# Reordering the start, the late modulation and the last attention heads of a fused adaLN attention and SwiGLU kernel

## Chip, cores and metric

The kernel runs on one core of one Trainium2 chip. The metric is device time in microseconds (us): the median of several executions. The profile of one execution gives the span, which is 1.8 us shorter than the timed value, and the start and duration of every instruction. It also records which share of its clock TensorE was granted; in these traces that is 1.0 or 0.5. TensorE is called PE, its weight loads PEld, VectorE DVE, ScalarE ACT, GpSimd POOL, and the queue that issues the transfers SP. An eviction is the copy of a finished result out of PSUM, where matmuls leave it; a load has landed when its data is there.

## The reference, cut to what matters

```python
mod = (silu(c) @ w_mod).reshape(1, 6, 1, -1)          # w_mod: 1024 x 6144
sa, ca, ga, sb, cb, gb = [mod[:, i] for i in range(6)]
h = layernorm(x) * (1 + ca) + sa                      # x: 2048 x 1024
q = h @ wq                                            # 32 heads of 128
#   softmax(q k^T / sqrt(128)) v over the last 512 cache rows, 4 kv heads
x = x + ga * (attention @ wo)
h = layernorm(x) * (1 + cb) + sb
x = x + gb * ((silu(h @ w_gate) * (h @ w_up)) @ w_down)   # 3584 wide
```

Here `s` stands for shift, `c` for scale and `g` for gate. Only `sa` and `ca` (16 columns of 128) are needed before the first query matmul. The other four (32 columns, "late modulation") are needed later: `ga` when the first chunk's attention is projected back, the rest only in the FFN.

## The kernel before

Rows are handled in four chunks of 512. Attention is one loop over 4 x 32 heads. In iteration i, PE projects the query of head i (`qproj`), computes the scores of head i-1, and multiplies the probabilities of head i-2 with V (`pv`); ACT does the exponentials between. After the last head of a chunk, `oproj` multiplies with `wo`. Every instruction goes through a helper that sets its semaphore waits in program order, and all transfers are issued by SP, one after the other.

The start: the modulation weights of `sa` and `ca` arrive as eight row blocks; row blocks of x are normalised and transposed between them; then the modulation is applied, and only head 0 is projected before the loop starts.

```python
for t in range(TPC):
    stats(t, t, 0); stats(t, t, 1); aggr(t)
    if t > 0:
        norm(t - 1, t - 1, t - 1)
        x_first(t - 1)
        mod_mm(wme[:, t - 1, :], B_wme[t - 1], t - 1, NE, XB)
# ... remaining blocks, mod_read, mod_gain, warm(4), modulate ...
qproj(0)
```

The late modulation: `ga` is done in chunk one with its own buffer. The rest goes through one single buffer in chunk two (heads 34 to 57), a load every third head, used two heads later.

```python
wml = h2s0[:, :, :].rearrange("p a b -> p (a b)")[:, 0:NL * P]      # the one buffer
def load_wml(k):
    T.op(Q_wml, lambda: SP.dma_start(wml, w_mod[k * P:(k + 1) * P, (NE + DT) * P:]), writes=[B_wml])
# ... in the loop over heads, at the head of iteration i ...
kk, odd = divmod(i - Hq - 2, 3)
if odd == 0 and 0 <= kk < DT:
    load_wml(kk)
if odd == 2 and 0 <= kk < DT:
    mod_mm(wml, B_wml, kk, NL, XB)          # 24 matmuls of one column
    # ... after the last: read, gain, row of gb ...
# ... if i > 0: qproj(i);  scores(i - 1);  pv(i - 2);  run_bg(1) ...
```

`run_bg` advances a background task, the layer norm of the next chunk. That task too issues transfers on SP: a DMA transpose of each normalised row block (L396), which waits for DVE. So does `pv`: it ends with a DMA transpose of the head's output (L567), which waits for its eviction by DVE.

The softmax here doesn't subtract the row's maximum and nothing guards it: scores larger than these inputs give would overflow.

Of the kernel before, what the change touches and what calls it, by code (L numbers as in the profile page):

```python
# [130 lines left out]
def bass_adaLN_cond__sliding_block_cached__swiglu_ffn__prompt_kernel(  # L131
# [49 lines left out]
    ident = S_("ident", [P, P], BF16)  # L181
    ones_bf = S_("ones_bf", [P, P], BF16)
# [7 lines left out]
    zwarm = S_("zwarm", [P, 512], BF16)  # L190
    rowb = [S_("rowb%d" % i, [P, D], BF16) for i in range(2)]
    diag = [S_("diag%d" % i, [P, P], BF16) for i in range(4)]
# [6 lines left out]
    h2s0 = S_("h2s0", [P, DT, CH], BF16)  # L199

    KB = 1024
    A_BYTES = 152 * KB
# [5 lines left out]
    ps_t = ps.tensor  # L208

# [14 lines left out]
    B_ident = _Buf("ident"); B_ones = _Buf("ones"); B_mh = _Buf("mhalf")  # L224
    B_cT = _Buf("cT"); B_sc = _Buf("sc"); B_modbf = _Buf("modbf"); B_c6 = _Buf("c6")
    B_mode = _Buf("mode"); B_modga = _Buf("modga"); B_gf = _Buf("gf"); B_zw = _Buf("zw")
    B_g = [_Buf("g%d" % i) for i in range(2)]
    B_row = [_Buf("row%d" % i) for i in range(2)]
    B_diag = [_Buf("diag%d" % i) for i in range(4)]
# [19 lines left out]
    with nc.Block() as block:  # L249

        @block.gpsimd
        def _(g):
# [9 lines left out]
            def transpose(out_ap, in_ap, reads, bank_buf):  # L262
                T.op(PE, lambda: TE.transpose(out_ap, in_ap, ident[:, :]),  # L263
                     reads=reads + [B_ident], writes=[bank_buf])
# [16 lines left out]
            T.op(POOL, lambda: g.memset(ident[:, :], 0.0), writes=[B_ident])  # L281
            T.op(POOL, lambda: g.affine_select(out=ident[:, :], in_=ident[:, :], compare_op=ALU.not_equal,
                                               fill=1.0, base=0, pattern=[[-1, P]], channel_multiplier=1),
                 reads=[B_ident], writes=[B_ident])
            T.op(POOL, lambda: g.memset(ones_bf[:, :], 1.0), writes=[B_ones])
            T.op(POOL, lambda: g.memset(mhalf[:, :], -0.5), writes=[B_mh])
            T.op(POOL, lambda: g.memset(zwarm[:, :], 0.0), writes=[B_zw])
# [25 lines left out]
            OFF_OS = 148 * KB  # L313
            OFF_KN = OFF_EX

            NE = 2 * DT
            B_wme = [_Buf("wme%d" % k) for k in range(DT)]
            wme = arena.at(OFF_OT, [DT, NE * P], BF16, [])
            arena.regs.append((OFF_OT, OFF_OT + 32 * KB, B_wme))
            Q_wm = [dq("q_wm%d" % k) for k in range(DT)]  # L320
            for k in range(DT):
                T.op(Q_wm[k], lambda: SP.dma_start(wme[:, k, :], w_mod[k * P:(k + 1) * P, 0:NE * P]), writes=[B_wme[k]])  # L322

            NWQ = 2
            B_wq = [_Buf("wq%d" % i) for i in range(NWQ)]
            wq_s = [arena.at(OFF_WQ + i * 8 * KB, [DT, 512], BF16, [B_wq[i]]) for i in range(NWQ)]
# [3 lines left out]
            def load_wq(gidx):  # L330
                if gidx >= NCH * HG:
                    return
                sl = gidx % NWQ
                hg = gidx % HG
                T.op(Q_wq[sl], lambda: SP.dma_start(  # L335
                    wq_s[sl], A_wq[:, hg * 512:(hg + 1) * 512].rearrange("(k p) n -> p k n", p=P)), writes=[B_wq[sl]])

            load_wq(0)
            B_kn = [_Buf("kn%d" % i) for i in range(Hkv)]
            B_kT = _Buf("kT"); B_va = _Buf("va")  # L340
            k_nat = arena.at(OFF_KN, [GK, P], BF16, B_kn)
            kT_sb = arena.at(OFF_KT, [GK, P], BF16, [B_kT])
# [5 lines left out]
            for gk in range(Hkv):  # L348
                T.op(Q_k[gk], lambda: SP.dma_start(k_nat[:, gk * KT:(gk + 1) * KT, :],
                                                   A_k_cache[0, gk, Sk - W:Sk, :].rearrange("(p k) d -> p k d", p=P)),  # L350
                     writes=[B_kn[gk]])
            for gk in range(Hkv):
# [4 lines left out]
            load_wq(1)  # L357
# [23 lines left out]
            def modulate(dst, bufs, dt, gi, ccol, cbuf):  # L381
                T.op(DVE, lambda: V.tensor_scalar(dst[:, dt, :], dst[:, dt, :], gain[gi][:, dt:dt + 1],  # L382
                                                  mod_bf[:, ccol + dt:ccol + dt + 1], op0=ALU.mult, op1=ALU.add),
                     reads=[B_g[gi], cbuf, bufs[dt]], writes=[bufs[dt]])
# [27 lines left out]
            def mod_mm(w_ap, wbuf, k, n, b):  # L412
                for j in range(n):
                    mm(bank(b, 1, 2 * j), w_ap[:, j * P:(j + 1) * P], sc_bf[:, k:k + 1],
                       k == 0 and j == 0, k == DT - 1, [wbuf, B_sc], PB[b], skip=True)

            def mod_read(b, jt0, n, cbuf):
                T.op(DVE, lambda: V.tensor_copy(mod_bf[:, jt0:jt0 + n], psap(b * 512, [[2, n]])),
                     writes=[PB[b], cbuf])

            def mod_gain(gi, jt, cbuf):
                T.op(DVE, lambda: V.tensor_scalar(gain[gi][:, :], mod_bf[:, jt:jt + DT], 1.0, None, op0=ALU.add),
                     reads=[cbuf], writes=[B_g[gi]])

            def warm(n):
                for _ in range(n):
                    mm(bank(QB), zwarm[:, 0:P], zwarm[:, :], True, True, [B_zw], PB[QB])


            def x_first(t):  # L430
                for dt in range(DT):
                    transpose(bank_bf(t)[:, dt * P:(dt + 1) * P], nsc4[t][:, dt * P:(dt + 1) * P], [B_ns4[t]], PB[t])
                T.op(ACT, lambda: A.activation(hT[0][:, :, t * P:(t + 1) * P],
                                               bank_bf(t).rearrange("p (a b) -> p a b", a=DT), AF.Copy),
                     writes=[PB[t]] + B_hT[0])

            for t in range(TPC):
                stats(t, t, 0)
                stats(t, t, 1)
                aggr(t)  # L440
                if t > 0:
                    norm(t - 1, t - 1, t - 1)
                    x_first(t - 1)
                    mod_mm(wme[:, t - 1, :], B_wme[t - 1], t - 1, NE, XB)
            norm(TPC - 1, TPC - 1, TPC - 1)
            x_first(TPC - 1)
            for k in range(TPC - 1, DT):
                mod_mm(wme[:, k, :], B_wme[k], k, NE, XB)
            mod_read(XB, 0, NE, B_mode)
            mod_gain(0, DT, B_mode)  # L450
            modulate(hT[0], B_hT[0], 0, 0, 0, B_mode)
            T.op(DVE, lambda: V.tensor_copy(gain_f[:, :], gain[0][:, :]), reads=[B_g[0]], writes=[B_gf])
            warm(4)
            for dt in range(1, 5):
                modulate(hT[0], B_hT[0], dt, 0, 0, B_mode)
            for dt in range(5, DT):
                T.op(ACT, lambda: A.activation(hT[0][:, dt, :], hT[0][:, dt, :], AF.Identity,
                                               bias=mod_bf[:, dt:dt + 1], scale=gain_f[:, dt:dt + 1]),
                     reads=[B_gf, B_mode, B_hT[0][dt]], writes=[B_hT[0][dt]])


            B_wga = [_Buf("wga%d" % k) for k in range(DT)]
            wga = arena.at(OFF_WO + 48 * KB, [DT, D], BF16, B_wga)
            Q_wga = [dq("q_wga%d" % i) for i in range(2)]

            def load_wga(i):
                hk = DT // 2
                T.op(Q_wga[i], lambda: SP.dma_start(
                    wga[:, i * hk:(i + 1) * hk, :],
                    w_mod[i * hk * P:(i + 1) * hk * P, NE * P:NE * P + D].rearrange("(k p) n -> p k n", p=P)),  # L470
                     writes=B_wga[i * hk:(i + 1) * hk])


            NL = NJ - NE - DT
            B_wml = _Buf("wml")
            Q_wml = dq("q_wml")
            for b_ in B_h2[0]:
                b_.absorb(B_wml)
            wml = h2s0[:, :, :].rearrange("p a b -> p (a b)")[:, 0:NL * P]

            def load_wml(k):
                T.op(Q_wml, lambda: SP.dma_start(wml, w_mod[k * P:(k + 1) * P, (NE + DT) * P:]), writes=[B_wml])


            def row_task(ri, jt, cbuf):
                T.op(POOL, lambda: g.tensor_copy(c6[:, jt:jt + DT], mod_bf[:, jt:jt + DT]), reads=[cbuf], writes=[B_c6])

                def diags(n):
                    for q in range(4):
                        col = jt + 4 * n + q  # L490
                        T.op(POOL, lambda: g.tensor_scalar(diag[q][:, :], ident[:, :], c6[:, col:col + 1], None, op0=ALU.mult),  # L491
# [4 lines left out]
                for n in range(2):  # L496
                    for q in range(4):
                        mm(bank(XB, P, q * P), ones_bf[:, :], diag[q][:, :], q == 0, q == 3, [B_ones, B_diag[q]], PB[XB], skip=True)
# [7 lines left out]
            NQT = 3; NEX = 2; NOS = 4  # L506
# [6 lines left out]
            def qproj(i):  # L513
# [4 lines left out]
                for kc in range(DT):  # L518
                    mm(bank(QB), wq_s[sl][:, kc, hh * P:(hh + 1) * P], hT[ch % 2][:, kc, :], kc == 0, kc == DT - 1,
                       [B_wq[sl], B_hT[ch % 2][kc]], PB[QB])  # L520
# [3 lines left out]
            qproj(0)  # L524
            for idx in range(GK):
                b = PVB + idx // 8
                transpose(bank_bf(b)[:, (idx % 8) * P:(idx % 8 + 1) * P], k_nat[:, idx, :], [B_kn[idx // KT]], PB[b])
            for bi in range(2):
                T.op(DVE, lambda: V.tensor_copy(kT_sb[:, bi * 8:bi * 8 + 8, :],
                                                bank_bf(PVB + bi).rearrange("p (a b) -> p a b", a=8)),  # L530
                     writes=[PB[PVB + bi], B_kT])
# [6 lines left out]
            def scores(i):  # L538
# [4 lines left out]
                for kt in range(KT):  # L543
                    mm(bank(SCB + kt), kT_sb[:, gk * KT + kt, :], qT_s[qs], True, True, [B_kT, B_qT[qs]], PB[SCB + kt])
# [43 lines left out]
            def oproj(ch):  # L588
                for k in range(2 * TPC):
                    j, hf = divmod(k, 2)  # L590
                    t = ch * TPC + j
                    b = [QB, XB][k % 2]
                    for h in range(Hq):
                        mm(bank(b), oT_all[:, h, j * P:(j + 1) * P], wo_s[h // 4][:, h % 4, hf * 512:(hf + 1) * 512],
                           h == 0, h == Hq - 1, [B_wo[h // 4], B_oT[h]], PB[b])
# [201 lines left out]
```

## Time and profile before

| | before |
|---|---|
| median of 4 runs | 1315.57 us (1314.04 to 1316.74) |
| span of the profiled run | 1314.7 us |
| PE busy | 97% |
| one 128x512 matmul to the next at full clock | 0.2157 us |
| the same with the clock not granted | 0.427 us |
| one 129-column matmul to the next | 0.0586 us |

PE is almost always busy, so the busy share says little. These are lines of the page of the kernel before: the span, busy times (share, instructions), and the granted clock of PE in 40 slices (9 is 90% or more).

```profile
span 1314.7 us, 18053 instructions
PE 1280.9 (97%) x7776; PEld 653.6 (50%) x7776; DVE 451.0 (34%) x827; ACT 339.0 (26%) x379; POOL 37.2 (3%) x92
PEclk9999999999999999999999999999999999999999
...
PE 94%; DMA 5%; SPq 1%; issue 0%; DVE 0%; ACT 0%; DVEq 0%
```

The last line is the chain of work that ended last, by engine. The 5% of DMA in it are the clue: something on PE waits for loads. The list of waits of PE in the kernel before shows which (total us, times, longest):

```profile
PE ps L259 <- DMA h2s<-in_w_mod_dram: 16.3, 7, 4.4
PE ps L263 <- DVE nsc L377: 8.0, 1, 8.0
PE ps L259 <- DMA arena<-in_w_mod_dram: 3.6, 4, 1.6
PE ps L259 <- DVE arena L564: 1.1, 1, 1.1
PE ps L259 <- DMA arena<-in_A_wq_dram: 0.7, 1, 0.7
PE ps L259 <- ACT arena L546: 0.4, 1, 0.4
```

The first line is the late modulation in its single buffer (`h2s`), the second the wait for the first normalised block at the start. The same by stretches of time, kernel before; columns are the stretch, its length, busy us (instructions) of PE, PEld, DVE, ACT and POOL, granted clock, DMA share and GB/s:

```profile
0.00:40.00 40.00, 27.21 (x270) 16.90 (x271) 16.70 (x35) 15.55 (x17) 5.10 (x18) 1.00 0.99 318
40.00:205.00 165.00, 165.00 (x1191) 91.66 (x1190) 70.13 (x136) 63.11 (x62) 8.29 (x17) 1.00 0.60 145
205.00:312.00 107.00, 90.66 (x815) 53.24 (x814) 45.18 (x94) 45.02 (x44) 4.68 (x12) 0.94 0.64 147
...
```

After the start, the stretch 205 to 312 is the only long one with an idle PE, and the only one with a clock below 1 (312 to 630, left out, is 318.00 busy of 318.00 at 1.00). The clock record of this trace begins with the first grant, at 27.43 us, so the 1.00 of the first row does not show the slow matmuls before it. A busy sum does not show the slow matmuls, so I used a finer account: every matmul is charged its interval at full clock (0.2157 us for 512 columns, 0.0586 for 129, 0.057 for a 128-column transpose, 0.025 for one column), and what lies between two starts beyond that is "lost". In stretches without stalls this account loses almost nothing: 0.01 us in the 165 us from 40 to 205 us. For the kernel before it gives 1266 us of pure matmul work and 48 us lost.

These are lines of SP and PE of the kernel before (start, us, what, wait before it and its cause):

```profile
220.87 0.75 PE L259 MATMUL ps<-sc_bf,h2s 128*128 128x1 bf16 x24 [2.10 <-DMA h2s<-in_w_mod_dram]
...
229.11 1.26 SPq L396 DMA_TRANSPOSE arena<-nsc  x1
230.46 0.53 SPq L335 DMA_DIRECT2D arena<-in_A_wq_dram  x1
231.04 0.63 SPq L482 DMA_DIRECT2D h2s<-in_w_mod_dram  x1
...
238.33 0.75 PE L259 MATMUL ps<-sc_bf,h2s 128*128 128x1 bf16 x24 [4.43 <-DMA h2s<-in_w_mod_dram]
```

The buffer is free at 221.6 us, but the next load is issued at 231.0 us. Before it in the queue stand the transpose of a head's output (L567, issued at 227.82 us after its wait for DVE), the transpose of the layer norm (L396) and a 1 MB load of `wq` (L335). It lands at 238.28 us, 7.2 us after its issue and 4.4 us after PE wanted it.

This is the start of the kernel before on PE (start, us, what, wait before it and its cause):

```profile
8.03 1.03 PE L263 MATMUL ps<-ident,nsc 128*128 128x128 bf16 x8 [8.03 <-DVE nsc L377]
...
20.01 1.87 PE L259 MATMUL ps<-zwarm 128*128 128x512 bf16 x4
22.62 3.59 PE L259 MATMUL ps<-arena 128*128 128x512 bf16 x8 [0.74 <-DMA arena<-in_A_wq_dram]
...
27.58 6.59 PE L259 MATMUL ps<-arena 128*128 128x512 bf16 x41
```

The eight query matmuls of head 0 take 3.59 us, 0.43 us each: the clock is not granted yet.

### The profile page before, as it was taken

The page shows a single profiled execution, that of the slowest core. Times are in us where ns is not written, and L with a number is a line of the kernel's source. Part 1 is how long each engine was busy: PE and PEld are TensorE (multiplying, and loading weights), DVE is VectorE, ACT ScalarE, POOL GpSimd, SP SyncE. Part 2 cuts the span into 40 slices and gives each one's busy share as a digit, 9 for nine tenths or more (in the row PEclk, how much of TensorE's full clock was granted, in tenths as well). Part 3 has the DMA queues.
Part 4 walks back from the last instruction along what each step waited for, and adds up shares of the span by engine and source line. Part 5 has one row for each costly group of instructions (what it writes and reads, how often), then busy time and mean ns, then how long its engine had stood idle before and what let it go on. Part 6 is the DMA issues. An engine that isn't in the chain of part 4 may idle for free.

```text
span 1314.7 us, 18053 instructions
## 1 busy us (share of the span) xinstructions
PE 1280.9 (97%) x7776; PEld 653.6 (50%) x7776; DVE 451.0 (34%) x827; ACT 339.0 (26%) x379; POOL 37.2 (3%) x92
## 2 busy tenths in 40 slices
PE   6999999879999999999999999999999999999999
PEld 3666545445545665455654444444444444444444
DVE  4555224444225543155431332223212332222112
ACT  3555204444204553045530111001110111001100
POOL 1010000001000000000000000000000000000000
PEclk9999999999999999999999999999999999999999
DMA  9998403775204643036460496025620574035400
GB/s 312 219 246 227 111 0 89 161 168 117 53 1 105 124 101 88 1 73 151 102 141 17 145 302 194 11 86 154 199 65 24 152 209 128 16 111 162 129 9 24
DMA packets 210560, 155.33 MB, mean 118 GB/s; under 512 B 104752, under 2 KB 195760, under 8 KB 210480
## 3 DMA queue, kind: packets, MB, share of 16 engines
q1 hardware_dynamic: 210480, 154.17, 44.2%
q8 instruction: 61, 1.00, 0.3%
q14 instruction: 19, 0.16, 0.0%
HBM read 125.83 MB, written 4.19 MB: 99 GB/s over the span
## 4 chain that ended last, share of the span: by engine, by line
PE 94%; DMA 5%; SPq 1%; issue 0%; DVE 0%; ACT 0%; DVEq 0%
PE ps L259 93%; DMA h2s<-in_w_mod_dram 3%; DMA arena<-in_A_wq_dram 1%; DMA arena<-in_B_w_up_dram 1%; SPq L322 0%; SPq L396 0%; PE ps L263 0%; SPq L302 0%; SPq L335 0%; ACT arena L546 0%; DVE arena L564 0%; DVE nsc L377 0%; SPq L683 0%; DVE tmp L583 0%; DVE arena L585 0%
## 5 line engine op out<-in xcount | busy, mean ns | idle before, releaser
L259 PE MATMUL ps<-arena 128*128 128x512 bf16 (+1 forms) x6428 | 1071.0, 329 | 2.3 <-DVE arena L564 1.1
L259 PEld LDWEIGHTS ps<-arena 128*128 128x128 bf16 x6428 | 549.7, 98 | 520.0 <-issue 9.2
L546 ACT ACTIVATE arena<-ps 128x1024 bf16<-128x1024 f32 x256 | 261.8, 1023 | 386.9 <-PE ps L259 375.2
L727 ACT ACTIVATE arena<-ps 128x512 bf16<-128x512 f32 x112 | 66.9, 597 | 520.2 <-PE ps L259 520.2
L259 PE MATMUL ps<-h2s,arena 128*128 128x512 bf16 x896 | 194.1, 379 | 0.3 <-DMA arena<-in_B_w_up_dram 0.3
L728 DVE TENSOR_TENSOR arena<-ps,arena 128x512 bf16<-128x512 f32 x112 | 77.5, 692 | 276.9 <-PE ps L259 276.9
L583 DVE TENSOR_TENSOR tmp<-ps,rowb 128x512 f32<-128x512 f32 (+1 forms) x65 | 44.4, 683 | 327.5 <-PE ps L259 327.5
L259 PEld LDWEIGHTS ps<-h2s,arena 128*128 128x128 bf16 x896 | 87.5, 98 | 106.5 <-DMA arena<-in_B_w_up_dram 1.3
L522 DVE CAST arena<-ps 128x512 bf16<-128x512 f32 x128 | 88.5, 692 | 92.8 <-PE ps L259 92.8
L564 DVE TENSOR_TENSOR arena<-ps,rl 128x512 bf16<-128x512 f32 x128 | 88.5, 691 | 4.6 <-DVE rl L561 0.2
L561 DVE RECIPROCAL rl<-ps 128x4 f32<-128x4 f32 x128 | 23.4, 183 | 143.6 <-PE ps L259 143.6
L366 DVE BATCH_NORM_STATS2 st<-x_res 128x6 f32<-128x512 bf16 x64 | 43.8, 684 | 4.4 <-DMA x_res<-in_A_x_dram 4.2
L371 POOL TENSOR_SCALAR rstd<-mv 128x1 f32<-128x1 f32 x32 | 7.7, 239 | 930.7 <-DVE mv L370 930.7
L585 DVE TENSOR_TENSOR arena<-tmp,x_res 128x512 bf16<-128x512 f32 (+1 forms) x33 | 22.3, 676 | 1.1
L585 DVE TENSOR_TENSOR x_res<-tmp,x_res 128x512 bf16<-128x512 f32 x32 | 22.1, 692 | 1.1
L259 PE MATMUL ps<-sc_bf,h2s 128*128 128x1 bf16 x192 | 6.1, 164 | 16.3 <-DMA h2s<-in_w_mod_dram 16.3
L373 POOL TENSOR_TENSOR rstd<-rstd,mhalf 128x1 f32<-128x1 f32 x32 | 18.2, 567 | 2.7
L382 DVE TENSOR_SCALAR arena<-arena,gain,mod_bf 128x512 bf16<-128x512 bf16 x45 | 16.3, 406 | 0.0
L377 DVE TENSOR_SCALAR nsc<-x_res,mv,rstd 128x1024 bf16<-128x1024 bf16 x30 | 16.0, 534 | 0.0
L259 PEld LDWEIGHTS ps<-sc_bf,h2s 128*128 128x128 bf16 x192 | 5.4, 97 | 17.6 <-DMA h2s<-in_w_mod_dram 17.6
L259 PE MATMUL ps<-sc_bf,arena 128*128 128x1 bf16 x192 | 7.4, 166 | 3.6 <-DMA arena<-in_w_mod_dram 3.6
L491 POOL TENSOR_SCALAR diag<-ident,c 128x128 bf16<-128x128 bf16 x16 | 9.7, 623 | 34.2 <-PE ps L259 33.9
(34 smaller groups left out, 53.6 us busy)
## 6 DMA issues: line engine op xcount, KB each, us to landing
arena<-in_A_wq_dram SPq DMA_DIRECT2D x32, 1024.0 KB, 6.1
arena<-in_B_w_gate_dram SPq DMA_DIRECT2D x28, 1024.0 KB, 5.6
arena<-in_B_w_up_dram SPq DMA_DIRECT2D x28, 1024.0 KB, 7.8
arena<-in_A_wo_dram SPq DMA_DIRECT2D x8, 1024.0 KB, 6.5
arena<-in_B_w_down_dram SPq DMA_DIRECT2D x7, 1024.0 KB, 6.1
h2s<-in_w_mod_dram SPq DMA_DIRECT2D x8, 768.0 KB, 5.4
arena<-in_w_mod_dram SPq DMA_DIRECT2D x8, 512.0 KB, 9.1
out_dram<-arena SPq DMA_DIRECT2D x15, 256.0 KB, 2.0
```

Source lines behind the costliest of these rows:

```text
L259: T.op(PE, lambda: TE.matmul(out_ap, lhsT, rhs, start=start, stop=stop, skip_group_check=skip), reads=reads, writes=[bank_buf])
L366: T.op(DVE, lambda: V.bn_stats(st_[sl][:, hf * 6:hf * 6 + 6], x_res[:, t, hf * 512:hf * 512 + 512]), reads=[B_x[t]], writes=[B_st[sl]])
L373: T.op(POOL, lambda: g.tensor_tensor(rstd[sl][:, :], rstd[sl][:, :], mhalf[:, 0:1], ALU.pow), reads=[B_rs[sl], B_mh], writes=[B_rs[sl]])
L382: T.op(DVE, lambda: V.tensor_scalar(dst[:, dt, :], dst[:, dt, :], gain[gi][:, dt:dt + 1], mod_bf[:, ccol + dt:ccol + dt + 1], op0=ALU.mult ...
L522: T.op(DVE, lambda: V.tensor_copy(qT_s[qs], bank(QB)), writes=[PB[QB], B_qT[qs]])
L546: T.op(ACT, lambda: A.activation(ex_s[es][:, 2 * kp:2 * kp + 2, :], banks2(SCB + 2 * kp), AF.Exp, scale=att_scale), writes=[PB[SCB + 2 * k ...
L561: T.op(DVE, lambda: V.reciprocal(rl[r][:, :].rearrange("p (a b) -> p a b", a=2), psap(PVB * 512 + P, [[512, 2], [130, 2]])), writes=both + ...
L564: T.op(DVE, lambda: V.tensor_tensor(o_s[os_].rearrange("p (a b) d -> p a b d", a=2), psap(PVB * 512, [[512, 2], [130, 2], [1, P]]), rlb, A ...
L583: T.op(DVE, lambda: V.tensor_tensor(tmp[s][:, 0:n], bank(b, n), rowb[ri][:, c0:c0 + n], ALU.mult), reads=[B_row[ri]], writes=[PB[b], B_tmp ...
L585: T.op(DVE, lambda: V.tensor_tensor(dst[:, c0:c0 + n], tmp[s][:, 0:n], x_res[:, t, c0:c0 + n], ALU.add), reads=[B_tmp[s], B_x[t]], writes= ...
L727: T.op(ACT, lambda: A.activation(sg_s[ss], bank(gb), AF.Silu), writes=[PB[gb], B_sg[ss]])
L728: T.op(DVE, lambda: V.tensor_tensor(guT[:, ft, :], bank(ub), sg_s[ss], ALU.mult), reads=[B_sg[ss]], writes=[PB[ub], B_gu[ft]])
```

## The change

Its intent, in three parts:

1. Start: `sa`/`ca` weights and `wq` arrive in halves of the contraction; the first four heads share each half as it lands, so three heads are projected ahead ("queries lead by three"). Row block 3 is normalised on ACT and POOL instead of DVE. The modulation is applied while evicting the transposes from PSUM.
2. Late modulation: all of it in chunk one, in eight buffers where `wo` will lie later; five heads between load and use.
3. End: as the queries lead by three, `oproj` matmuls of the last chunk fill the last heads' iterations.

The core of the diff (helpers, allocations and evictions cut):

```diff
+            for sl in range(2):
+                load_wme(sl)          # 4 transfers: shift and scale, each in two contraction halves
+                load_wq0(sl)          # half of wq's first group
...
+            tl = TPC - 1
+            T.op(ACT, lambda: A.activation(nsc4[tl], x_res[:, tl, :], AF.Copy, accum_out=acc[:, 0:1]), ...)
+            T.op(POOL, lambda: g.tensor_scalar(nmean[:, :], acc[:, 0:1], -1.0 / D, None, op0=ALU.mult), ...)
+            T.op(ACT, lambda: A.activation(nsc4[tl], x_res[:, tl, :], AF.Square, bias=nmean[:, 0:1], accum_out=acc[:, 1:2]), ...)
+            stats(0, 0, 0); stats(0, 0, 1); aggr(0)      # aggr: rstd on POOL
+            stats(1, 1, 0); stats(1, 1, 1); aggr(1)
+            norm(0, 0, 0); x_first(0); mod_slice(0, 0)
+            ... norm(1, 1, 1); x_first(1); norm(2, 2, 2); mod_slice(0, 1); x_first(2); x_first(3); x_mod(0)
...
-            qproj(0)
+            QB0 = [QB, PVB, PVB + 1, SCB]
+            LEAD = 3
+            for sl in range(2):
+                if sl == 1:
+                    warm(4, SCB + 1)
+                    mod_slice(1, 0)
+                    warm(2, SCB + 1)
+                    mod_slice(1, 1)
+                    x_mod(1)
+                for kc in range(sl * HK, (sl + 1) * HK):
+                    for h in range(LEAD + 1):
+                        mm(bank(QB0[h]), wq_s[0][:, kc, h * P:(h + 1) * P], hT[0][:, kc, :], kc == 0, kc == DT - 1, ...)
...
-            wml = h2s0[:, :, :].rearrange("p a b -> p (a b)")[:, 0:NL * P]
+            wml = [arena.at(OFF_WO + k * 8 * KB, [NL * P], BF16, [B_wml[k]]) for k in range(DT)]
-            LOADX = {0: 1, 13: 2, 21: 3}
+            LOADX = {3: 1, 19: 2, 40: 3}
+            LOADM = {1 + (3 * k) // 2: k for k in range(DT)}
+            MODM = {6 + (3 * k) // 2: k for k in range(DT)}
+            LOADO = {16 + (15 * p) // 8: p for p in range(8)}
...
+                if i + LEAD < NA:
+                    qproj(i + LEAD)
                 if 0 <= i - 1 < NA:
                     scores(i - 1)
+                n = i - (NA - LEAD)
+                if 0 <= n <= 2:
+                    oproj_mm(NCH - 1, 0, QB, 8 * n, 8 * n + 8)
+                elif n == 3:
+                    oproj_mm(NCH - 1, 1, XB, 0, 12)
                 if 0 <= i - 2 < NA:
                     pv(i - 2)
...
-            oproj(NCH - 1)
+            HL = Hq - 4
+            oproj_mm(NCH - 1, 1, XB, 12, HL)
+            oproj_mm(NCH - 1, 0, QB, 24, HL)
+            oproj_mm(NCH - 1, 2, SCB, 0, HL)
+            for k, b in ((0, QB), (1, XB), (2, SCB)):
+                oproj_mm(NCH - 1, k, b, HL, Hq)
+                oproj_end(NCH - 1, k, b)
+            oproj(NCH - 1, 3)
```

## The prediction

> **What bounds it now.** TensorE: the chain of waits gives PE 94% of a 1314.7 us span. Back-to-back 128x512 matmuls start (timeline) every 0.2157 us, 129-column ones every 0.0586 us. Charging every matmul this interval, I get about 1266 us of pure matmul work and 48 us lost, in five places:
> - Start, 19.2 us: first PE work at 8.0 us, then waits, and eight query matmuls at 0.43 us each (clock not granted); steady from 27.6 us.
> - 215 to 309 us, 23.4 us: PE waits for the modulation weights in their single buffer seven times (16.3 us in the list of waits); after the longer waits the matmuls are again 0.43 us apart. Window table: 77.9 busy of 94.2 us, clock 0.93.
> - End of attention, 1.9 us: 0.6 on an exponential near 671 us, 1.25 on DVE at 674.6 (the last PV waits for the eviction before it).
> - FFN 0.7 us, tail 3.1 us.
> Elsewhere every gap is nominal: a longer query lead buys nothing.
>
> **Late modulation to chunk one.** Eight buffers, five heads (18 us) from load to use; a 1 MB load lands in 6 to 12. All 23.4 us should go. The price is 6 MB more DMA in chunk one, which already shows a share near 1.0 from 50 to 100 us; weights in long packets move at about 400 GB/s (2.6 us per MB, in 5.4 us of heads). I allow 0.4 us of new stall.
>
> **Start.** The chain is longer: POOL runs in order and the new mean (input at 7.2 us, ACT 1.0 us) stands before the first rstd, so the first norm moves from 7.5 to about 9.6 us; PE then has four groups of transposes (1.0 each) and two modulation slices (1.2 each) in series: 16.5 us; then sixteen query matmuls from about 17.1 us, 8 to 16 of them at 0.43 us. The Trainium skill, "TensorE: Matmul & The Clock Gate", Part 1, says a free-running window of about 3.4 us of sustained activity must pass; the trace agrees (0.43 us spacing until 27.4 us, slow stretches of 3.4 and 6.8 us after the stalls). After the second slice and 1.4 us of DVE work the second half starts near 27.2 us (26.5 to 28.5). DMA (1 KB instead of 4 KB packets, 46 against 159 ns each: 15% slower) ends at about 22 us and isn't the limit. Nominal work done by then: 9.8 us, so 17.4 us is lost, plus 0.6 for the exponential's table load: 18.0 against 19.2. Gain about 1, not the 5 that three extra heads suggest.
>
> **End of attention.** The fill takes the 0.6; the last PV still directly follows the one before it: 1.25 stays.
>
> **Sum.** 1315.8 - 23.4 - 1.2 - 0.6 + 0.4 (stall) + 0.4 (two more warm matmuls) = 1291.4. I say 1291 us, 8 in 10 between 1286 and 1296. Chances: faster by over 2% 0.38, within 2% 0.61, slower 0.01. The 2% line is at 1289.5.
>
> **Right if:** no wait for late modulation weights on PE, clock 1.0 after 30 us; attention ends 24 us earlier; the second half's query matmuls start at 26.5 to 28.5 us; one PV wait of about 1.2 us at the end; FFN length unchanged.
>
> **Wrong if:** the clock is granted earlier in the first half (3 to 4 us gained); transposes queue behind chunk one's loads so that DVE, then PE, stalls; waits in the start let the clock fall again.

## The result, and the profile after

| | before | after |
|---|---|---|
| median | 1315.57 us (4 runs) | 1291.83 us (4 runs, 1290.49 to 1292.60) |
| span of the profiled run | 1314.7 us | 1290.8 us |
| ratio after / before | | 0.982, 95% interval 0.980 to 0.984 |

A ratio is the mean time of one kernel's runs over that of the other's of the same rounds, so it is not quite the ratio of the medians quoted. Executions over 1.5% slower than the fastest of the same kernel are left out of the means. The kernel is 24 us faster, 1.8%, which is within 2%.

The page of the changed kernel:

```profile
span 1290.8 us, 17912 instructions
PE 1265.6 (98%) x7636; PEld 651.7 (50%) x7778; DVE 447.7 (35%) x823; ACT 341.3 (26%) x384; POOL 37.3 (3%) x94
PEclk9999999999999999999999999999999999999999
...
PE 97%; issue 1%; DVE 1%; ACT 0%; DMA 0%; SPq 0%; POOL 0%; ACTq 0%
```

This trace lacks about 140 matmul records (7636 against 7778 weight loads), so its PE sums are some 8 us short (1262.6 us up to 1285 us, against 1271.0 in the complete trace after_look). Among dense matmuls at full clock a missing record is a gap of two intervals, and the account of lost time counts it as a matmul; where the clock is halved such a gap (0.431 us) looks almost like a normal interval (0.427), and there the weight loads and the total tell. DMA has left the chain. The waits of PE in the changed kernel:

```profile
PE ps L270 <- DVE nsc L399: 10.2, 1, 10.2
PE ps L266 <- DVE arena L467: 2.2, 2, 1.7
PE ps L266 <- DVE arena L638: 1.1, 1, 1.1
PE ps L266 <- ACT arena L620: 0.6, 2, 0.4
PE ps L266 <- DVE tmp L657: 0.4, 1, 0.4
```

No load is waited for. In place of it the wait for the first block grew from 8.0 to 10.2 us, and there is a new one on DVE L467 (the modulation of the second half). The stretches of a third trace of the same changed kernel, which has all its records (labelled after_look below), over the same times as before:

```profile
0.00:40.00 40.00, 27.87 (x265) 16.30 (x266) 13.99 (x32) 15.40 (x19) 5.23 (x20) 0.96 0.85 288
40.00:205.00 165.00, 165.00 (x1366) 94.52 (x1364) 70.48 (x137) 63.49 (x62) 13.18 (x26) 1.00 0.70 186
205.00:312.00 107.00, 107.00 (x836) 63.24 (x835) 55.84 (x112) 58.65 (x58) 3.17 (x8) 1.00 0.53 123
...
```

Between 205 and 312 us PE is now fully busy at full clock. Chunk one takes the added 6 MB (DMA share 0.60 to 0.70) without one idle moment of PE. But the first stretch has a clock of 0.96: it was taken away once more after the first grant. The start on PE, changed kernel:

```profile
10.24 1.03 PE L270 MATMUL ps<-arena,nsc 128*128 128x128 bf16 x8 [10.24 <-DVE nsc L399]
...
16.30 6.08 PE L266 MATMUL ps<-arena 128*128 128x512 bf16 x19 [0.47 <-DVE arena L467]
...
23.44 0.94 PE L266 MATMUL ps<-sc_bf,arena 128*128 128x1 bf16 x32
26.10 5.30 PE L266 MATMUL ps<-arena 128*128 128x512 bf16 x16 [1.71 <-DVE arena L467]
```

The record of the first query matmul is missing: its weight load stands at 15.89 us and the next at 15.92. So the first half starts at 15.92 us, not at 16.30, and the 0.47 us printed there is no wait. The sixteen query matmuls of the second half need 5.30 us instead of 3.6 (3.61 us in slice_early below): the clock, granted at 19.95 us, was taken away again from 26.8 to 30.2 us.

The account of lost time, three traces of each kernel (the two further ones of before and the third of after come from the last experiment), in us:

| stretch | before | mean | after | mean |
|---|---|---|---|---|
| start, up to 40 us | 19.2, 17.0, 17.5 | 17.9 | 18.5, 17.8, 17.5 | 17.9 |
| late modulation, 205 to 312 | 23.5, 22.4, 22.9 | 22.9 | 0.0, 0.0, 0.0 | 0.0 |
| end of attention, 630 to 690 | 1.9, 1.9, 1.9 | 1.9 | 2.4, 2.4, 2.4 | 2.4 |
| FFN (0.4 of it is rounding) | 1.1, 1.7, 2.0 | 1.6 | 0.4, 0.4, 0.4 | 0.4 |
| tail | 3.1 | 3.1 | 3.1 | 3.1 |
| span | 1314.7, 1312.1, 1313.4 | 1313.4 | 1290.8, 1290.1, 1289.8 | 1290.3 |

The spans differ by 23.1 us. The late modulation alone accounts for 22.9 of it, the FFN for 1.2; the start gives nothing, the end gives back 0.6, and the two added warm-up matmuls cost 0.4. Some expectations below quote earlier counts of the start, which took slow intervals for missing records or the reverse: recounted, 18.9 and 18.0 (changed kernel) are 18.5 and 17.8, and 16.8 (late_alone) is 17.5.

### The profile page after: what moved, and what is told of

Its sections match the earlier page's. It is cut to its first block, busy times and chain, and to the rows that moved or that the text cites. A ratio compares the mean times of both kernels' runs of the same rounds, so it can differ in the third digit from the quotient of the medians.

```text
span 1290.8 us, 17912 instructions
## 1 busy us (share of the span) xinstructions
PE 1265.6 (98%) x7636; PEld 651.7 (50%) x7778; DVE 447.7 (35%) x823; ACT 341.3 (26%) x384; POOL 37.3 (3%) x94
## 4 chain that ended last, share of the span: by engine, by line
PE 97%; issue 1%; DVE 1%; ACT 0%; DMA 0%; SPq 0%; POOL 0%; ACTq 0%
PE ps L266 97%; DMA x_res<-in_A_x_dram 0%; ACT arena L620 0%; PE ps L270 0%; DVE tmp L657 0%; DVE arena L467 0%; DVE st L388 0%; ACT L620 0%; ACT arena L489 0%; SPq L309 0%; DVE nsc L399 0%; DVE arena L638 0%; DVE x_res L659 0%; ACT arena L593 0%; DVE rl L635 0%
## 5 line engine op out<-in xcount | busy, mean ns | idle before, releaser
L266 PE MATMUL ps<-arena 128*128 128x512 bf16 (+1 forms) x7204 | 1251.5, 333 | 12.0 <-DVE arena L467 2.2
L266 PEld LDWEIGHTS ps<-arena 128*128 128x128 bf16 x7346 | 637.4, 98 | 624.9 <-issue 7.9
L571 DVE CAST arena<-ps 128x512 bf16<-128x512 f32 x124 | 85.8, 692 | 65.5 <-PE ps L266 65.5
L635 DVE RECIPROCAL rl<-ps 128x4 f32<-128x4 f32 x128 | 23.4, 183 | 149.7 <-PE ps L266 149.7
L404 DVE TENSOR_SCALAR arena<-arena,gain,mod_bf 128x512 bf16<-128x512 bf16 x56 | 20.4, 406 | 0.0
L270 PE MATMUL ps<-arena,nsc 128*128 128x128 bf16 x16 | 2.1, 311 | 10.4 <-DVE nsc L399 10.2
L266 PEld LDWEIGHTS ps<-sc_bf,arena 128*128 128x128 bf16 x384 | 11.3, 97 | 0.5
L266 PE MATMUL ps<-sc_bf,arena 128*128 128x1 bf16 x384 | 11.5, 164 | 0.0
L540 POOL TENSOR_SCALAR arena<-arena,c 128x128 bf16<-128x128 bf16 x16 | 9.7, 621 | 36.0 <-PE ps L266 35.9
L392 DVE BATCH_NORM_AGGREGATE mv<-st 128x2 f32<-128x12 f32 x31 | 6.5, 209 | 1.1
```

What stands on the lines that cost most here:

```text
L266: T.op(PE, lambda: TE.matmul(out_ap, lhsT, rhs, start=start, stop=stop, skip_group_check=skip), reads=reads, writes=[bank_buf])
L404: T.op(DVE, lambda: V.tensor_scalar(dst[:, dt, :], dst[:, dt, :], gain[gi][:, dt:dt + 1], mod_bf[:, ccol + dt:ccol + dt + 1], op0=ALU.mult ...
L571: T.op(DVE, lambda: V.tensor_copy(qT_s[qs], bank(QB)), writes=[PB[QB], B_qT[qs]])
L635: T.op(DVE, lambda: V.reciprocal(rl[r][:, :].rearrange("p (a b) -> p a b", a=2), psap(PVB * 512 + P, [[512, 2], [130, 2]])), writes=both + ...
```

## The experiments

Theory A: the gain is the removal of the waits for late modulation weights and of the halved clock after them; the new start and the end fill bring nothing. Theory B: the start brings 3 us or more, and chunk one's extra loads take part of it back. The first four kernels ran on one chip with five rounds and shared nine runs of the kernel before; the next four likewise.

### The changed kernel again

No edit; the yardstick of the first four.

> The changed kernel once more, as the yardstick for the other runs of this call: 1292 us, ratio to the kernel before 0.982, and again about 18.9 us lost on TensorE up to 40 us, none in the late modulation, 1.85 us at the end of attention.

Measured: 1291.44 us, ratio 0.9816 (0.9802 to 0.9830), as expected. Its losses are in the table above: none in the late modulation, 17.8 us at the start, and 2.4 us at the end, where 1.85 was expected.

### Late modulation alone

The kernel before, with part 2 and nothing else:

```diff
-            wml = h2s0[:, :, :].rearrange("p a b -> p (a b)")[:, 0:NL * P]
+            NL = NJ - NE
+            wml = [arena.at(OFF_WO + k * 8 * KB, [NL * P], BF16, [B_wml[k]]) for k in range(DT)]
+            LOADX = {3: 1, 19: 2, 40: 3}
+            LOADM = {1 + (3 * k) // 2: k for k in range(DT)}
+            MODM = {6 + (3 * k) // 2: k for k in range(DT)}
+            LOADO = {16 + (15 * p) // 8: p for p in range(8)}
... (the separate ga path is dropped, both rows are made after the last matmul, add_ln1 at head 8)
```

> The kernel before with nothing but the late modulation moved to chunk one in eight buffers. Theory A (nearly all of the gain is the seven waits for modulation weights and the halved clock after them; the new start and the fill of the last heads bring about nothing): the 23.4 us between 215 and 309 us vanish, so 1292 to 1293 us, within 1.5 us of the changed kernel. Theory B (the shared first heads bring 3 us or more, and the added loads in chunk one take something back): at least 3 us slower than the changed kernel, 1295 us or more, or new TensorE gaps of over 0.3 us between 40 and 200 us.

Measured: 1293.25 us, ratio 0.983 (0.9814 to 0.9845); lost in the late modulation 0.0 us, at the start 17.5, at the end 1.9, in the FFN 2.2. No gap over 0.3 us between 40 and 640 us. It is 1.8 us behind the changed kernel of the same call, between what A (1.5) and B (3) allowed, but the intervals overlap, and its trace says what the difference is: the FFN lost 1.8 us more than in the changed kernel, the start 0.3 us less (after_again: 17.8). So the start is not what puts it behind. Theory A holds; one part of three carries the gain.

### The load one head earlier, nothing else moved

A kernel with a second buffer in chunk two did not build for want of memory. So the single buffer stayed, and only the place of the load in the loop changed, from the start of the third iteration to right behind the matmuls that free the buffer:

```diff
-                    if odd == 0 and 0 <= kk < DT:
-                        load_wml(kk)
                     if odd == 2 and 0 <= kk < DT:
                         mod_mm(wml, B_wml, kk, NL, XB)
+                    if odd == 2 and 0 <= kk + 1 < DT:
+                        load_wml(kk + 1)
+                    if odd == 2 and 0 <= kk < DT:
                         if kk == DT - 1:
```

> The kernel before, single buffer and chunk two kept, but each load of late modulation weights is issued right after the matmuls that free the buffer: three heads from issue to use instead of two. Theory A1 (what stalled was the distance from issue to use, about 3 us too short): each wait shrinks by one head, 3.5 us, so of 2.3, 4.6, 2.0, 2.5, 1.3, 4.2 and 0.7 us there remain 1.1 and 0.7 us, the clock stays at full, and the time is 1293 to 1297 us. Theory A2 (one buffer, or the place in chunk two, is what costs): most of the waits stay and the time is over 1303 us.

Measured: 1292.95 us, ratio 0.9827 (0.9812 to 0.9842). The late modulation loses nothing any more; the start lost 18.8 us, the FFN 2.1. SP and PE in this run, to be held against the lines of the kernel before:

```profile
218.21 0.74 PE L259 MATMUL ps<-sc_bf,h2s 128*128 128x1 bf16 x24
...
220.92 0.53 SPq L482 DMA_DIRECT2D h2s<-in_w_mod_dram  x1
...
224.75 1.26 SPq L396 DMA_TRANSPOSE arena<-nsc  x1
...
229.38 0.74 PE L259 MATMUL ps<-sc_bf,h2s 128*128 128x1 bf16 x24
```

The load now stands before both transposes of this head and before the load of `wq`. It is issued 2.7 us after the matmuls that use the buffer start, not 10.2 us (220.87 to 231.04 before), lands at 225.65 us, 4.7 us after its issue, and is used at 229.38 us. I had expected the waits to shrink by one head (3.5 us) and 1.8 us to remain, on the two longest. They vanished, because the load left more behind than one head. In the kernel before, four of the seven late loads stand behind a layer norm transpose (1.3 to 1.9 us of the queue each), and all seven behind a transpose of a head's output. SP's own list of waits from 205 to 312 us shows 2.2 us in all before L396 and 85.6 us before L567, so it is mostly the latter that waits for DVE. And the two longest waits (4.4 and 4.0 us) belong to the two loads that follow directly on a load of `wq`: these landed 7.2 and 8.2 us after their issue, the other five after 5.1 to 5.9. One head earlier no load of `wq` stands directly before these two, and they land in 4.7 and 4.6 us; two others now follow a load of `wq` and land in 7.2 us, still 0.9 us before their use. The run moves all of this together; what each is worth alone was not tested. The Trainium skill, "DMA: Bandwidth & Descriptors", section on the anatomy of one DMA, says that DMA engines do not wait on semaphores and that a wait happens on the issuing sequencer before dispatch; these two traces agree: the load is issued only after the transposes before it have ended their waits. Its rules for kernel authors advise to issue a DMA early and to wait late; here that was worth nearly the whole gain, 22.6 us by the medians, with neither more buffers nor a move to another chunk.

### The order on POOL

The changed kernel, with the new mean behind the first two rstd:

```diff
-            T.op(POOL, lambda: g.tensor_scalar(nmean[:, :], acc[:, 0:1], -1.0 / D, None, op0=ALU.mult), ...)
-            T.op(ACT, ... AF.Square ...)
             stats(0, 0, 0); stats(0, 0, 1); aggr(0)
             stats(1, 1, 0); stats(1, 1, 1); aggr(1)
+            T.op(POOL, lambda: g.tensor_scalar(nmean[:, :], acc[:, 0:1], -1.0 / D, None, op0=ALU.mult), ...)
+            T.op(ACT, ... AF.Square ...)
             norm(0, 0, 0)
```

> The changed kernel with the mean of row block 3 put behind the two first rstd on POOL. If POOL's order delayed the start, the first transpose comes at about 8 instead of 10.2 us; the first half of the query matmuls is then held by the modulation weights (first slice landed at 13.0 us) and starts near 15.4 instead of 16.3 us, the second near 25.2 instead of 26.1 us; about 1291 us, 1 us faster than the changed kernel. If the loads set the start, nothing changes after 13 us.

Measured: 1292.01 us, ratio 0.9819 (0.9805 to 0.9833), no faster than the changed kernel (0.9816). The first transpose does come at 7.8 instead of 10.3 us, but PE then waits for the modulation weights, as its list of waits shows:

```profile
PE ps L270 <- DVE nsc L399: 7.8, 1, 7.8
...
PE ps L266 <- DMA arena<-in_w_mod_dram: 1.8, 2, 1.0
```

The first half starts at 15.35 us, 0.6 us earlier than in after_again (15.94; in both the first record is missing), the second at 24.64 against 25.42. Of 2.5 us gained at the head, 1.8 go into waits for loads. POOL's order was a delay, as predicted. The start of this trace loses 16.9 us against 17.8, but the timing of the five rounds shows nothing of it.

### Warm-up matmuls in the gap of the second half

```diff
                     mod_slice(1, 1)
+                    warm(8, SCB + 1)
                     x_mod(1)
```

> The changed kernel with eight more warm-up matmuls (1.7 us) behind the second modulation slice, in the 1.9 us in which TensorE waits for the modulation of the second half. If that idle time lets the clock fall, all sixteen query matmuls of the second half now run at 0.216 us (3.5 us instead of 4.9) and the kernel gains 1.5 to 1.9 us, 1290 us. If the one-column matmuls of the slices count as idle for the clock, it still falls and nothing is gained (1292 us).

Measured: 1290.43 us, ratio 0.9802 (0.9784 to 0.9820); span 1288.8 against 1289.8 to 1290.8 of three traces of the changed kernel. The second half on PE, warm8:

```profile
23.07 0.94 PE L266 MATMUL ps<-sc_bf,arena 128*128 128x1 bf16 x32
23.88 5.46 PE L266 MATMUL ps<-arena 128*128 128x512 bf16 x23
```

The clock stays granted from 19.3 us on: 24 matmuls (one record is missing) follow at 0.216 us, with one gap of 0.13 us. So the clock does not fall without the idle 1.9 us: filling it removes the slow stretch. What the one-column matmuls before it add to the fall is not shown. The lost time at the start falls from 17.9 to 14.7 us, but 1.7 us of the difference is the added warm-up work. The time is 1.4 us below the changed kernel's median; with these intervals that alone would not prove a gain. The clock record shows that the slow stretch is gone.

### The second modulation slice earlier

Its weights landed at 19.8 us and were used at 23.4.

```diff
                 if sl == 1:
-                    warm(4, SCB + 1)
-                    mod_slice(1, 0)
-                    warm(2, SCB + 1)
-                    mod_slice(1, 1)
+                    warm(3, SCB + 1)
                     x_mod(1)
                 for kc in range(sl * HK, (sl + 1) * HK):
+                    if kc == HK - 1:
+                        mod_slice(1, 0)
+                        mod_slice(1, 1)
```

> The changed kernel with the second modulation slice moved ahead of the last four query matmuls of the first half (its weights landed at 19.8 us but were used at 23.4 us). DVE's work on the slice is then covered by four matmuls and three warm-ups: the second half starts near 24.1 instead of 26.1 us and stays at full clock; 3.5 to 4.5 us gained, about 1288 us. If the loads hold the start, the second half still starts near 26 us.

Measured: 1288.43 us, ratio 0.9784 (0.9765 to 0.9802). PE at the start, slice_early:

```profile
15.85 3.38 PE L266 MATMUL ps<-arena 128*128 128x512 bf16 x11 [0.47 <-DVE arena L467]
19.07 1.74 PE L266 MATMUL ps<-sc_bf,arena 128*128 128x1 bf16 x64
20.89 1.46 PE L266 MATMUL ps<-arena 128*128 128x512 bf16 x6
22.82 3.61 PE L266 MATMUL ps<-arena 128*128 128x512 bf16 x16 [0.47 <-DVE arena L467]
```

The first of the twelve matmuls is again missing, so the first half starts at 15.47 us. The second half starts at 22.8 us, earlier than the 24.1 expected, mostly because the clock came at 17.6 us in this run, and takes 3.61 us. The start loses 14.2 us. This is the gain that the shared heads were meant to bring: not more heads, but the dependent slice ahead of the work that can hide it.

### The end fill ahead of the scores

In the changed kernel the fill stands behind `scores`, but what PE waits for are the banks that `scores` writes. And `pv` of the last head still follows directly on the one before. These are the gaps of the changed kernel at the end of attention:

```profile
642.85 14.71 PE L266 MATMUL ps<-arena 128*128 128x512 bf16 x112 [0.43 <-ACT arena L620]
658.65 14.04 PE L266 MATMUL ps<-arena 128*128 128x129 bf16 x74 [1.09 <-DVE arena L638]
673.08 3.20 PE L266 MATMUL ps<-arena 128*128 128x512 bf16 x14 [0.39 <-DVE tmp L657]
```

The edit:

```diff
-                if 0 <= i - 1 < NA:
-                    scores(i - 1)
                 n = i - (NA - LEAD)
                 if 0 <= n <= 2:
                     oproj_mm(NCH - 1, 0, QB, 8 * n, 8 * n + 8)
                 elif n == 3:
-                    oproj_mm(NCH - 1, 1, XB, 0, 12)
+                    oproj_mm(NCH - 1, 1, XB, 0, 8)
+                elif n == 4:
+                    oproj_mm(NCH - 1, 1, XB, 8, 16)
+                if 0 <= i - 1 < NA:
+                    scores(i - 1)
...
-                    b = [QB, XB][k % 2]
+                    b = [QB, XB][(k + k0) % 2]     # the fourth group goes to the bank evicted first
```

> The changed kernel with the output matmuls put ahead of the scores instead of behind them, eight of them between the last two PV groups, and the fourth output group in the bank that is evicted first. If the three end gaps (0.59 us on an exponential, 1.25 us on the PV eviction, 0.55 us on a residual) are a matter of placement, all three vanish: 2.4 us gained, about 1289.5 us. If the fill was off the path anyway, no gain.

Measured: 1289.28 us, ratio 0.9794 (0.9775 to 0.9812); lost at the end 0.0 instead of 2.4 us. The waits of PE in this run (all four) have no entry of the end left:

```profile
PE ps L270 <- DVE nsc L399: 10.2, 1, 10.2
PE ps L266 <- DVE arena L467: 2.2, 2, 1.7
PE ps L266 <- ACT arena L620: 0.2, 1, 0.2
PE ps L266 <- DMA arena<-in_w_mod_dram: 0.2, 1, 0.2
```

The placement was the fault, as expected: the same matmuls in another order close all three gaps.

### The three together

> The changed kernel with the POOL order, the early slice and the end fill together. First half at about 15.4 us, second half near 23.5 us at full clock, no gap at the end: about 7 us faster than the changed kernel, 1285 us (1283.5 to 1287), ratio to the kernel before 0.976 to 0.978.

The edits of pool_first, slice_early and end_fill in one kernel. Measured: 1285.88 us, ratio 0.9767 (0.9749 to 0.9785). It beats both kernels, as expected in size, and it is the only kernel whose whole interval lies below 0.98. The end loses 0.0 us, the start 15.4, the FFN nothing beyond the rounding. The first half starts at 15.84 us instead of the 15.4 expected, since PE now waits for the modulation weights (1.06 and 0.88 us before it, 1.04 us in the second slice): with the order on the engines mended, the transfers hold the start.

### How much the start varies

Two more traces of the kernel before and one of the changed one, one look each, so their state is unknown; only the accounts of lost time are used.

> The kernel before, unchanged, for one more profile of its start. So far the time lost on TensorE up to 40 us was 19.2, 16.8 and 18.8 us with the old start (before, late_alone, early_load) and 18.9, 18.0 and 18.5 us with the new one (changed kernel twice, end_fill). If the new start brings nothing, this falls between 16.5 and 19.5 us; if it brings 2 us or more, the old start should lie at 20 us or above. The late modulation should lose 21 to 25 us again.

> The same again: 16.5 to 19.5 us lost up to 40 us if the new start brings nothing, 20 us or more if it does.

> The changed kernel, unchanged, for a third profile of its start: 17.5 to 19 us lost up to 40 us, with the second half of the query matmuls at 0.43 us again, if the lost clock there is not a chance of one run.

Measured: 17.0 and 17.5 us lost at the start of the kernel before, 17.5 us in the changed one; the late modulation of the kernel before lost 22.4 and 22.9 us. Over all traces the old start lost 17.0 to 19.2 us (five traces), the new one 17.5 to 18.5 us (four, with end_fill's 18.5). The new start is no better. In all four the second half's matmuls were slow. Theory B has fallen.

## Why the prediction was right or wrong

- **The total** (1291 predicted, 1291.8 measured) and "within 2%" came out, and for the main reason given: the 23.4 us of the late modulation are gone to the last tenth, no new stall arose in chunk one (0.4 allowed, 0.0 found), the first FFN activation comes at 709.6 instead of 732.8 us. That the sum fits to 0.8 us is partly luck: start and end each came out 1.2 us worse than predicted, against which the FFN gave 1.2 us and chunk one's stall 0.4 us that were not counted on.
- **"The second half starts near 27.2 us (26.5 to 28.5)" failed.** It started at 26.1, 25.4 and 25.1 us in three traces. The step that failed first is the chain before the query matmuls: the first half started at 15.92, 15.94 and 15.67 us, not near 17.1, because a group of eight transposes delayed the next work by 0.83 us and not 1.0, and a slice by 0.9 to 1.2. From the first half to the second it took 10.2, 9.5 and 9.5 us, where 10.1 were predicted. The clock was granted 4.0, 2.6 and 2.6 us after the first query matmul, where 3.4 to 6.8 was assumed; this accounts for the shorter two. That the transposes and one-column matmuls before them count in part would explain the early grants, and so would the free-running window that the prediction quotes; neither was tested alone.
- **"Waits in the start let the clock fall again"** stood under what would make the prediction wrong, and it happened, in all three traces of the changed kernel, in end_fill and in pool_first. In all five the clock fell 6.8 us after it was granted (at 26.78 us after 19.95 in the first), twice the 3.4 us for which it stayed away. The second half lost about 1.7 us there (5.30 us for sixteen matmuls instead of 3.6). So the 18.0 us predicted to be lost at the start (17.9 measured) came out by luck: the early start and the second loss of the clock cancelled. The gain of about 1 us did not come: three traces of before also lose 17.9 us in the mean, of which only the slowest, 19.2, was known.
- **POOL's order** was read rightly from the code: the first norm moved to 9.64 us (9.6 predicted). But it did not set the start alone; without it the loads hold PE for 1.8 of the 2.5 us. "DMA isn't the limit" was true of the kernel as it was, not of the next one.
- **"The fill takes the 0.6" failed.** The wait for the exponential moved three heads earlier, to 642 us, because the fill stands behind the scores, and the new order of the last groups added 0.55 us for an eviction. The 1.25 us of the last PV stayed, as predicted.
- **"FFN 0.7 us", unchanged, was mis-sized.** The FFN lost 0.7 to 1.8 us beyond rounding in all five traces of the kernel before and its two variants, and 0.0 to 0.1 in seven of the eight traces of the changed kernel and its variants, but 1.4 in slice_early. The waits are for gate and up weights near 1034 to 1064 us, and in four of the traces also near 762 to 788 us. The FFN's code is the same in all. What decides between the two stays open.

## What to carry to other kernels

Where one queue issues all transfers in program order, the place of a load in the program is a time: put it right behind the last use of its buffer, ahead of any transfer that waits for an engine and not directly behind another large load, before spending memory on more buffers. A fill only fills if it stands in front of the instruction that waits, not behind it. Count a stall of PE together with the slow matmuls after it, and when two parts of a change are meant to help, run the one with the large wait alone first.

## What the Trainium skill lacked or had wrong

- "TensorE: Matmul & The Clock Gate", table on why this matters, advises against PE-idle gaps of more than about 3 us. Here 1.9 us idle, after 0.9 us of one-column matmuls, took the clock away for 3.4 us in every one of five traces that had this gap (three of the changed kernel, end_fill, pool_first), while in the first trace of the kernel before two waits of 2.0 and 2.5 us after dense matmuls (at 251 and 264 us) did not, and one of 2.3 us (at 218 us) did. In before_look1 the clock did fall at the wait near 263 us, so the same gap can go either way. The page does not say how one-column matmuls count; with eight dense warm-ups in the gap the clock stayed.
- The same page, Part 1, gives about 3.4 us of sustained activity before the clock is granted. Measured from the first dense 512-column matmul it took 4.0, 2.6 and 2.6 us in three traces of the changed kernel, and 2.1 us in slice_early, with transposes and one-column matmuls ahead of them. The page calls the window free-running, so some scatter is what it says.
- "DMA: Bandwidth & Descriptors", specifications, gives 512 B as the least transfer for line rate. In the packet records of the kernel before, a 1 KB packet took 46 ns and a 4 KB packet 159 ns in the median; on 16 engines that is 356 against 412 GB/s, so 1 KB is still about 14% short.
- No page says that a load can be late merely because of what stands before it in the issuing queue: DMA transposes that wait for an engine, or a large load. The first follows from the remark on the sequencer in "DMA: Bandwidth & Descriptors". Together with the halved clock after the waits, the late place of these loads cost 22 us here.
